# Part of VectorE's score tiles in the third bank of a score unit, and a corrected row-group duration in the planner

## The chip, the cores and the metric

The kernel runs on one core of a Trainium2 chip. Five engines work side by side: TensorE (PE for its matmuls, PEld for its weight loads), VectorE (DVE), ScalarE (ACT), GpSimd (POOL) and SyncE (SP), which issues the DMAs. Matmul results go to eight PSUM banks of 512 fp32 columns per partition. The metric is the device time of one execution in microseconds (us); lower is better.

## The reference

One pre-layernorm transformer block over 2048 tokens of width 640, in bf16: attention with 32 heads of 20 channels, then a gated GELU feed-forward (FFN) of width 1728, each with a residual.

```python
def _A_ref(x, wqkv, wo):
    qkv = (lambda x, *d: x.transpose(*d))((x @ wqkv).reshape(B, S, 3, H, Dh), 2, 0, 3, 1, 4)
    q, k, v = qkv[0], qkv[1], qkv[2]
    scores = jnp.einsum("bhqd,bhkd->bhqk", q, k) * (Dh ** -0.5)
    p = _softmax(scores, axis=-1)
    o = jnp.einsum("bhqk,bhkd->bhqd", p, v)
    return (lambda x, *d: x.transpose(*d))(o, 0, 2, 1, 3).reshape(B, S, D) @ wo
def _B_ref(x, w_gate, w_up, w_down):
    g = jnp.einsum("bsd,df->bsf", x, w_gate)
    u = jnp.einsum("bsd,df->bsf", x, w_up)
    return jnp.einsum("bsf,fd->bsd", _gelu(g) * u, w_down)
h = x + _A_ref(_layernorm(x, axis=-1), A_wqkv, A_wo)
h2 = h + _B_ref(_layernorm(h, axis=-1), B_w_gate, B_w_up, B_w_down)
```

## The kernel before

**Tiles.** The queries are cut into eight chunks (SIZES: one of 512, five of 256, two of 128 rows). Heads go in eight groups of four; the four heads of a group sit in four row groups of TensorE (32 rows each), so their score matmuls can run at the same time. A score tile is 128 keys by 512 columns of one head: one PSUM bank. A *slot* is as many head groups as fill 512 columns for a chunk (one group at 512 queries, two at 256, four at 128): 32 slots of 64 tiles, 2048 tiles in all.

**Two ways to an exponential.** Most tiles are taken in *units* that alternate between banks 0, 1, 2 and banks 3, 4 (PAT, line 829). One score operation on TensorE fills a unit's banks, and one ScalarE instruction (line 1002) takes the exponential of all of them into the probability buffers pts and pts2 (the latter a part of the buffer that the profile calls rege). The rest, D_SLOT quads of four tiles per slot, go to VectorE (d_exp, lines 880 to 908). A VectorE tile's scores are computed by a score operation of their own into a *background bank*, 7 or 5 (BG, line 1232; unit, lines 995 to 998), just behind the unit with which it is due. VectorE reads the bank (line 887), which frees it, into a quarter of a scratch tile; after four such tiles it makes four scaled copies (TERMS) that together approximate the exponential. SUMS says how many pairs of copies in a slot are added up first, so that they need one PV pass instead of two.

**PV and epilogue.** PV passes add probability times value into bank 6 (pv_op). When a slot is complete, VectorE copies bank 6 out (epilogue), and spread (lines 1021 to 1040) sends the softmax sums through four DMA hops and a reciprocal on GpSimd, multiplies on VectorE (on16, priority P_ON) and writes to the tensor attn. After the last slot of a chunk, post (line 1099) adds the output projection, the layer norm and the FFN for that chunk's rows as background work. Its accumulators use the background banks too. The FFN matmuls stand at line 674 in narrow column groups of 32 (chunks of 512 and 256 rows) and at lines 1156 and 1221 at full width (chunks of 128).

**The planner.** No order of an engine is written out by hand. Every operation is given a priority, a duration, its inputs and the banks that it takes and frees. Sched.schedule (lines 97 to 259) plays the engines forward in time and always starts the ready operation of best priority; this makes each engine's instruction order, which emit writes out with the semaphores needed. On the chip each engine follows that fixed order, whatever its real times are. What matters here: MODE_SWITCH is added on TensorE when it changes between row groups, column groups and the full array; row_start and row_end (lines 220 to 231) follow the four row groups, so that a tile for a free row group costs nearly nothing; SD_AGE (line 156) holds back a background score tile for a while so that it can join a unit; due and QK_LEAD keep background work from starting when the next unit's banks are about to come free; HOP is the time that the planner gives to one DMA hop of spread. When TensorE has nothing to do, the planner adds warm matmuls on kt_all.

Of the kernel before, what the change touches and what calls it, by code (L numbers as in the profile page):

```python
# [22 lines left out]
PE_AGE = 3.5  # L23
SD_AGE = 0.6

MODE_SWITCH = {"pe": .098, "act": 1.28}
# [20 lines left out]
class Sched:  # L49
# [47 lines left out]
    def schedule(self):  # L97
# [11 lines left out]
        mode = {e: None for e in ENGINES}  # L109
# [6 lines left out]
        t = 0.0  # L116
        recent = collections.deque()
        row_end, row_start, freed = [0.0] * 4, 0.0, [0.0] * 8
# [3 lines left out]
        scores = sum(o.eng == "pe" and o.mode == "row" for o in ops)  # L122
        while done < total:
            assert events, "no operation can start"
            t = heapq.heappop(events)
            while events and events[0] <= t + 1e-9:
                heapq.heappop(events)
            for e in ENGINES:
# [8 lines left out]
                while ready[e]:  # L137
# [10 lines left out]
                    for bk in o.acq:  # L148
# [4 lines left out]
                        else:  # L153
                            got = None
                            break
                    if got and 0 < p[0] < 1 and mode[e] != "row" and t - o.ready < SD_AGE and scores > 1:
                        skipped.append((p, i))
                        continue
# [63 lines left out]
                if o.rows:  # L222
                    if mode[e] == "row":
                        b = max([row_start + 0.01] + [freed[x.b] for x in o.acq] + [row_end[j] for j in o.rows])
                    else:
                        row_end = [0.0] * 4
                        b = t
                    row_start = b
                    for j in o.rows:
                        row_end[j] = b + 0.215  # L230
                    o.dur = max(0.012, b + 0.215 - t)
                if e == "act":
# [114 lines left out]
PR, PR2 = 12, 4  # L347
D_SLOT = (0,) + (3,) * 27 + (2,) * 2 + (1,) * 2
SUMS = (0, 1, 1, 1, 0) + (1,) * 20 + (2, 1, 0, 1, 0, 1, 0)
HOP = 2.6  # L350
D_LAT = 0.3
RECIP_MAGIC = float(0x7EF311C3)
COL = 256
VN = 6
SIX = ()
D_FIRST, D_SPAN = 0, 16
TANH_FROM = 768
# [6 lines left out]
P_KQ = 3  # L364
P_ON = 2
V_ACT = (0, 1)
# [5 lines left out]
def bass_sequential_preLN__mha_block__glu_gated_geglu__prompt_kernel(  # L372
# [12 lines left out]
    with ExitStack() as es:  # L385
# [442 lines left out]

        PAT = [((0, 1, 2), (3, 4, 5)) if c in SIX else ((0, 1, 2), (3, 4)) for c in range(len(CHUNKS))]
        d_kb, d_sums, n_sums = {}, {}, {}  # L830
# [8 lines left out]
        d_rem = {s_: [(s_,) + y + (j,) for y in ys for j in range(4)] for s_, ys in d_kb.items()}  # L839
        units, ubank, dtile, uslot = [], [], [], []  # L840
        in_slot = {}
        while rem:
            s_ = rem[0][0]
            c = slots[s_][0]
            bs = PAT[c][len(units) % 2]
            k = in_slot.setdefault(s_, [0, 0])
            nd = 4 * len(d_kb[s_])
            six = len(PAT[c][1]) == 3
            want = min(nd, (k[0] - D_FIRST) * nd // D_SPAN + 1) if k[0] >= D_FIRST and nd else 0
            xd = None  # L850
            n = len(bs)
            if k[1] < want:
                n -= six
                xd = d_rem[s_].pop(0)
                k[1] += 1
            units.append(rem[0:n])
            del rem[0:n]
            ubank.append(bs[0])
            dtile.append(xd)
            uslot.append(s_)  # L860
            k[0] += 1
# [18 lines left out]
        def d_exp(b, tile, prio):  # L880
# [7 lines left out]
                                                                 ALU.mult, ALU.max), c_dve(512), P_QK,  # L888
                            reads=[("SD", tile)], writes=[vk], rel=[b], after=aft))
            d_raw.append(tile)  # L890
# [4 lines left out]
            for i, off in enumerate(TERMS):  # L895
                a, ak = d_a[e][d_t[e] % len(d_a[e])]
                d_t[e] += 1
                d_ops.append(op("dve", I("tensor_scalar", a, v, 0.25, off, ALU.mult, ALU.add), 0.6, prio,
                                reads=[vk], writes=[ak], after=aft, lat=D_LAT))
                if i // 2 < pairs:  # L900
# [49 lines left out]
        def unit(u):  # L950
# [11 lines left out]
            xd = dtile[u]  # L962
            six = xd and len(PAT[slots[tl[0][0]][0]][1]) == 3
            al = tl + ([xd] if six else [])
# [357 lines left out]
```

## Time and profile before

| | us |
|---|---|
| median of 3 runs | 886.22 (883.67 to 892.12) |
| the profiled execution | 887.99 |
| its span, first to last instruction | 886.2 |
| TensorE's granted clock, mean | 0.998 |

The profile is of one execution. In the rows, L393 is the line of a helper that records every plain operation, so such rows are told apart by their tiles: pts<-ps and rege<-ps at 128x1024 or 128x1536 on ACT are exponentials of two or three banks, rege<-rege and qt_all<-... at 128x2048 on DVE are VectorE's scaled copies (parts of qt_all serve as scratch once their queries are used up), ps<-pts,v_all on PE is PV, on<-osb,bsum is the normalising multiply of spread. L974 is a score matmul, L887 is VectorE's read of a score bank. A timeline row merges consecutive instructions of one group: start, length to the end of the last, and in brackets how long the engine was idle before and what ended that.

### The profile page before, as it was taken

How to read it: one execution, taken by the hardware profiler on the slowest of the kernel's cores; microseconds unless marked ns; L12 is line 12 of the kernel's file. 1: busy time of each engine (PE TensorE's matmuls, PEld its weight loads, DVE VectorE, ACT ScalarE, POOL GpSimd, SP SyncE). 2: the span in 40 equal slices, each digit the busy share in tenths (PEclk: the TensorE clock that was granted, in tenths of full speed). 3: DMA queues.
4: the chain of work that ended last, by engine and by line, in shares of the span. 5: the costliest groups of instructions: out<-in, count | busy, mean ns of one | idle time of the engine just before them, and what ended most of it. 6: DMA issues, size and time to landing. Idle time of an engine off the chain costs nothing.

```text
span 886.2 us, 36314 instructions
## 1 busy us (share of the span) xinstructions
PE 839.1 (95%) x16536; PEld 416.4 (47%) x16536; DVE 746.2 (84%) x1340; ACT 838.5 (95%) x766; POOL 131.8 (15%) x431
## 2 busy tenths in 40 slices
PE   3999999999989899999999999999999999999998
PEld 1532222222234344434555555555555556666776
DVE  8838998899879988878899988899999988947753
ACT  6799999999989999999999999999999999999962
POOL 5001011110111311110031211130111211110100
PEclk9999999999999999999999999999999999999999
DMA  7211121322264510001112100201011111021000
GB/s 267 79 46 58 30 74 31 97 67 61 67 148 142 146 34 20 18 7 34 50 41 57 34 19 15 55 20 34 20 41 42 22 36 43 24 50 43 11 18 16
DMA packets 57297, 46.93 MB, mean 53 GB/s; under 512 B 25524, under 2 KB 50704, under 8 KB 57144
## 3 DMA queue, kind: packets, MB, share of 16 engines
q1 hardware_dynamic: 57144, 44.62, 19.0%
q8 instruction: 129, 2.11, 1.0%
q14 instruction: 24, 0.20, 0.1%
HBM read 30.68 MB, written 11.04 MB: 47 GB/s over the span
## 4 chain that ended last, share of the span: by engine, by line
ACT 47%; PE 41%; DVE 8%; DMA 2%; issue 1%; SPq 1%; DVEq 0%
ACT pts L393 35%; PE ps L974 13%; ACT rege L393 11%; PE ps L674 11%; PE ps L393 10%; PE ps L679 5%; PE ps L1156 1%; DVE rege L393 1%; DVE rege L887 1%; DVE stats L393 1%; PE ps L1221 1%; ACT qt_all L393 1%; DMA bsum<-rsums 1%; SPq L393 1%; DVE qt_all L393 1%
## 5 line engine op out<-in xcount | busy, mean ns | idle before, releaser
L393 ACT ACTIVATE pts<-ps 128x1024 bf16<-128x1024 f32 (+1 forms) x567 | 642.8, 1255 | 13.1 <-PE ps L974 8.1
L974 PE MATMUL ps<-qt_all,kt_all 32*128 32x256 bf16 (+2 forms) x4096 | 320.3, 273 | 15.5 <-ACT pts L393 8.8
L974 PEld LDWEIGHTS ps<-qt_all,kt_all 32*128 32x128 bf16 x4096 | 115.9, 92 | 217.1 <-ACT pts L393 110.9
L393 ACT ACTIVATE rege<-ps 128x1536 bf16<-128x1536 f32 x113 | 170.9, 1512 | 1.5 <-PE ps L974 0.9
L887 DVE TENSOR_SCALAR rege<-ps 128x512 int16<-128x512 f32 x216 | 147.4, 683 | 28.8 <-PE ps L974 27.6
L674 PE MATMUL ps<-rege,regw 128*32 128x256 bf16 (+1 forms) x3360 | 150.3, 292 | 2.0 <-DVE rege L887 0.5
L393 PE MATMUL ps<-pts,v_all 128*21 128x256 bf16 (+2 forms) x2752 | 133.7, 273 | 0.6 <-issue 0.5
L393 PE MATMUL ps<-rege,v_all 128*21 128x256 bf16 (+2 forms) x1828 | 126.2, 289 | 3.7 <-DVE rege L393 3.3
L887 DVE TENSOR_SCALAR qt_all<-ps 128x512 int16<-128x512 f32 x132 | 90.4, 685 | 23.5 <-PE ps L974 22.6
L674 PEld LDWEIGHTS ps<-rege,regw 128*32 128x32 bf16 x3360 | 79.0, 96 | 36.8 <-issue 17.6
L393 POOL TENSOR_SCALAR rn<-rc 128x16 int32<-128x16 int32 x30 | 9.3, 311 | 576.4 <-DMA rc<-sums 576.2
L393 DVE TENSOR_SCALAR rege<-rege 128x2048 int16<-128x2048 int16 x138 | 92.6, 686 | 1.5 <-PE ps L393 0.6
L679 PE MATMUL ps<-regw 128*128 128x512 bf16 (+1 forms) x360 | 87.8, 352 | 2.9 <-ACT regw L626 2.0
L393 PEld LDWEIGHTS ps<-pts,v_all 128*21 128x21 bf16 x2752 | 62.7, 92 | 32.2 <-issue 26.7
L674 PE MATMUL ps<-regw,rege 128*32 128x320 bf16 x1568 | 74.4, 301 | 1.6 <-issue 0.5
L393 DVE TENSOR_SCALAR qt_all<-qt_all 128x2048 int16<-128x2048 int16 (+3 forms) x116 | 68.2, 597 | 1.5 <-PE ps L393 0.7
L393 PEld LDWEIGHTS ps<-rege,v_all 128*21 128x21 bf16 x1828 | 48.3, 91 | 40.4 <-issue 20.3
L393 PE MATMUL ps<-qt_all,v_all 128*21 128x256 bf16 (+1 forms) x1280 | 58.0, 266 | 1.0 <-issue 0.7
L393 DVE TENSOR_SCALAR qt_all<-rege 128x2048 int16<-128x2048 int16 x80 | 54.4, 688 | 1.4 <-PE ps L393 0.7
L679 PEld LDWEIGHTS ps<-regw 128*128 128x128 bf16 x360 | 28.9, 98 | 49.9 <-issue 27.7
L674 PEld LDWEIGHTS ps<-regw,rege 128*32 128x32 bf16 x1568 | 36.1, 96 | 21.2 <-issue 10.4
L1209 DVE TENSOR_TENSOR rege<-rege,ps 128x512 bf16<-128x512 bf16 (+1 forms) x53 | 35.8, 676 | 7.6 <-PE ps L674 7.3
(115 smaller groups left out, 705.7 us busy)
## 6 DMA issues: line engine op xcount, KB each, us to landing
bsum<-rsums SPq DMA_DIRECT2D x120, 64.0 KB, 2.1
rege<-in_A_x_dram SPq DMA_DIRECT2D x5, 640.0 KB, 5.6
q_rows<-regw SPq DMA_DIRECT2D x20, 128.0 KB, 1.8
out_dram<-rege SPq DMA_DIRECT2D x16, 160.0 KB, 2.4
attn<-on SPq DMA_DIRECT2D x120, 20.0 KB
regw<-in_B_w_gate_dram SPq DMA_DIRECT2D x5, 432.0 KB, 3.4
regw<-in_B_w_up_dram SPq DMA_DIRECT2D x5, 432.0 KB, 3.2
kt_all<-k_rows SPq DMA_DIRECT2D x12, 160.0 KB
```

Of the source, the lines that this page charges most:

```text
L393: return lambda eng: getattr(eng, method)(*args, **kwargs)
L674: return [lambda eng, j=j: eng.matmul(out()[32 * j:32 * j + 32], l[:, 32 * j:32 * j + 32], r, start=start, stop=stop, tile_position=(0, 32 ...
L679: fn = col4(lambda: bank(bk, n), l, r, k == 0, k == len(steps) - 1) if col else lambda eng, l=l, r=r, k=k: eng.matmul(bank(bk, n), l, r, s ...
L887: d_ops.append(op("dve", lambda eng: eng.tensor_scalar(v[:, 512 * h:512 * h + 512], bank(b), EXP_MUL, -32000.0, ALU.mult, ALU.max), c_dve( ...
L974: return lambda eng: eng.matmul(out()[:, kk * nq:(kk + 1) * nq], kt_all[32 * j:32 * j + 32, g, kt * 128:(kt + 1) * 128], qt_all[32 * j:32 ...
L1156: lambda eng, a=a, f=f, fi=fi: eng.matmul(bank(bk)[:, fi * nq:(fi + 1) * nq], w[:, a, F0[f]:F0[f] + 128], hnT[:, a, 128 * tb:128 * tb + nq ...
L1209: hdone.append(op("dve", lambda eng, bu=bu, fv=fv, w=w: eng.tensor_tensor(fv, fv, bank(bu, w), ALU.mult), c_dve(w), p, reads=[ku] + hkeys( ...
L1221: f == NF - 1) if nq >= COL else lambda eng, f=f, o=o, hf=hf, bk=bk: eng.matmul(
```

## The change

- unit: where a VectorE tile is due in a three-bank unit, the unit may take two ScalarE tiles and have the VectorE tile in its third bank, computed in the same score operation. A list ring holds for which units this is so. D_RING gives a number per slot; out of a slot's 4 x D_SLOT tiles it spreads that many marks, and a marked tile takes the third bank if its unit has three banks; if not, it goes to a background bank as before. It replaces SIX, an empty list that would have added a sixth bank.
- d_exp: the scratch tile is tracked by quarters.
- schedule: when a score operation starts from another array mode, its rows are now counted from after the mode change and not from before it; the time of the operation itself stays the same. The rule that holds back background score tiles gets a second limit SD_ROW for when the array is in row mode.
- Constants: D_SLOT (87 to 89 quads), SUMS (28 pairs, distributed over other slots), HOP 2.6 to 3.2, P_ON 2 to 2.4, D_SPAN 16 to 18 (over how many units of a slot the VectorE tiles are spread).

Reads and writes otherwise stay as they are, but since the planner makes every order anew, all engines' orders differ from an early point on.

```diff
@@ -22,6 +22,7 @@
 QK_LEAD = .65
 PE_AGE = 3.5
 SD_AGE = 0.6
+SD_ROW = 0
 
 
 
@@ -153,7 +154,8 @@
                         else:
                             got = None
                             break
-                    if got and 0 < p[0] < 1 and mode[e] != "row" and t - o.ready < SD_AGE and scores > 1:
+                    if got and 0 < p[0] < 1 and scores > 1 and t - o.ready < (
+                            SD_AGE if mode[e] != "row" else SD_ROW if row_end[o.rows[0]] > max([row_start + 0.01] + [freed[b] for b in got]) + 0.02 else 0):
                         skipped.append((p, i))
                         continue
                     if got is None:
@@ -224,11 +226,11 @@
                         b = max([row_start + 0.01] + [freed[x.b] for x in o.acq] + [row_end[j] for j in o.rows])
                     else:
                         row_end = [0.0] * 4
-                        b = t
+                        b = t + (MODE_SWITCH[e] if mode[e] else 0.0)
                     row_start = b
                     for j in o.rows:
                         row_end[j] = b + 0.215
-                    o.dur = max(0.012, b + 0.215 - t)
+                    o.dur = max(0.012, b + 0.215 - t) - (b - t if mode[e] not in (None, "row") else 0.0)
                 if e == "act":
                     due = t + o.dur + (0.905 if o.dur > 1.2 else 1.332) - QK_LEAD if o.mode == "exp" else None
                 if o.util:
@@ -345,15 +347,15 @@
 NTERM = len(TERMS)
 PV_QUADS = 2
 PR, PR2 = 12, 4
-D_SLOT = (0,) + (3,) * 27 + (2,) * 2 + (1,) * 2
-SUMS = (0, 1, 1, 1, 0) + (1,) * 20 + (2, 1, 0, 1, 0, 1, 0)
-HOP = 2.6
+D_SLOT = (0,) + (3,) * 27 + (2, 3, 2, 1)
+SUMS = (0,) + (1,) * 6 + (0, 1, 1, 0) + (1,) * 5 + (2,) + (1,) * 10 + (0, 1, 1, 1, 0)
+HOP = 3.2
 D_LAT = 0.3
 RECIP_MAGIC = float(0x7EF311C3)
 COL = 256
 VN = 6
-SIX = ()
-D_FIRST, D_SPAN = 0, 16
+D_RING = (6,) * 26 + (4, 6, 12, 12, 0, 6)
+D_FIRST, D_SPAN = 0, 18
 TANH_FROM = 768
 GELU_A = 2.0 * 0.7978845608028654
 GELU_B = 4.0 * GELU_A * 0.044715
@@ -362,7 +364,7 @@
 P_EV = 1.8
 P_QK, P_PV, P_TAIL, P_PRO, P_EPI, P_LN, P_BG = 0, 1, 1.2, 1.5, 2, 2.5, 3
 P_KQ = 3
-P_ON = 2
+P_ON = 2.4
 V_ACT = (0, 1)
 XN_DVE = (9, 13, 15)
 V0 = 0
@@ -826,7 +828,7 @@
             tiles += [(s_, g, kb, j) for g in gs for kb in range(NT // nk) for j in range(4)]
             slot_end.append(len(tiles))
 
-        PAT = [((0, 1, 2), (3, 4, 5)) if c in SIX else ((0, 1, 2), (3, 4)) for c in range(len(CHUNKS))]
+        PAT = [((0, 1, 2), (3, 4)) for c in range(len(CHUNKS))]
         d_kb, d_sums, n_sums = {}, {}, {}
         for s_, (c, gs) in enumerate(slots):
             mine = list(dict.fromkeys(x[1:3] for x in tiles if x[0] == s_))
@@ -837,7 +839,7 @@
             n_sums[s_] = k
         rem = [x for x in tiles if x[1:3] not in d_kb[x[0]]]
         d_rem = {s_: [(s_,) + y + (j,) for y in ys for j in range(4)] for s_, ys in d_kb.items()}
-        units, ubank, dtile, uslot = [], [], [], []
+        units, ubank, dtile, uslot, ring = [], [], [], [], []
         in_slot = {}
         while rem:
             s_ = rem[0][0]
@@ -845,12 +847,12 @@
             bs = PAT[c][len(units) % 2]
             k = in_slot.setdefault(s_, [0, 0])
             nd = 4 * len(d_kb[s_])
-            six = len(PAT[c][1]) == 3
             want = min(nd, (k[0] - D_FIRST) * nd // D_SPAN + 1) if k[0] >= D_FIRST and nd else 0
             xd = None
             n = len(bs)
+            ring.append(k[1] < want and n == 3 and (k[1] + 1) * D_RING[s_] // max(nd, 1) > k[1] * D_RING[s_] // max(nd, 1))
+            n -= ring[-1]
             if k[1] < want:
-                n -= six
                 xd = d_rem[s_].pop(0)
                 k[1] += 1
             units.append(rem[0:n])
@@ -886,7 +888,7 @@
             aft = tuple(e_ops) + (tuple(last_qk[0]) if qb else ()) + (tuple(last_qk[1]) if qb > 1 else ())
             d_ops.append(op("dve", lambda eng: eng.tensor_scalar(v[:, 512 * h:512 * h + 512], bank(b), EXP_MUL, -32000.0,
                                                                  ALU.mult, ALU.max), c_dve(512), P_QK,
-                            reads=[("SD", tile)], writes=[vk], rel=[b], after=aft))
+                            reads=[("SD", tile)], writes=[vk + (h,)], rel=[b], after=aft))
             d_raw.append(tile)
             if h < 3:
                 return
@@ -896,7 +898,7 @@
                 a, ak = d_a[e][d_t[e] % len(d_a[e])]
                 d_t[e] += 1
                 d_ops.append(op("dve", I("tensor_scalar", a, v, 0.25, off, ALU.mult, ALU.add), 0.6, prio,
-                                reads=[vk], writes=[ak], after=aft, lat=D_LAT))
+                                reads=[vk + (k,) for k in range(4)], writes=[ak], after=aft, lat=D_LAT))
                 if i // 2 < pairs:
                     if i % 2 == 0:
                         m, mk = a, ak
@@ -960,7 +962,7 @@
             pb, o = (pts, p0) if p0 < PR else (pts2, p0 - PR)
             pt = pb[:, 512 * o:512 * (o + na)]
             xd = dtile[u]
-            six = xd and len(PAT[slots[tl[0][0]][0]][1]) == 3
+            six = ring[u]
             al = tl + ([xd] if six else [])
             bks = [Bank(s0 + i) for i in range(len(al))]
             fns = []
```

## The prediction

> **What bounds the kernel now.** I read the page first, then three stretches of the span, then ScalarE alone between its first and its last exponential.
>
> ```profile
> span 886.2 us, 36314 instructions
> PE 839.1 (95%) x16536; PEld 416.4 (47%) x16536; DVE 746.2 (84%) x1340; ACT 838.5 (95%) x766; POOL 131.8 (15%) x431
> ...
> ACT 47%; PE 41%; DVE 8%; DMA 2%; issue 1%; SPq 1%; DVEq 0%
> ```
>
> TensorE and ScalarE both look full, and the chain of waits runs through both. The stretches (length, then busy time of PE, PEld, DVE, ACT, POOL) part them:
>
> ```profile
> 35.70:851.00 815.30, 788.04 (x15881) 378.94 (x15881) 697.05 (x1200) 802.83 (x707) 119.66 (x399) 1.00 0.19 49
> 851.00:886.20 35.20, 30.27 (x506) 25.43 (x502) 18.75 (x44) 11.21 (x15) 0.00 (x0) 1.00 0.06 20
> ```
>
> From 35.7 to 851 ScalarE has a record open for 802.8 of 815.3 us. Behind that comes a tail of 35.2 us in which it does little and TensorE is busy for 30.3. So the time is a ScalarE stage plus a TensorE tail. ScalarE's groups in the stage (count | union of records, mean ns of one | idle before):
>
> ```profile
> L393 ACT ACTIVATE pts<-ps 128x1024 bf16<-128x1024 f32 x340 | 369.5, 1087 | 4.3 <-PE ps L393 3.3 <-PE ps L974 0.8
> L393 ACT ACTIVATE pts<-ps 128x1536 bf16<-128x1536 f32 x227 | 342.0, 1506 | 8.9 <-PE ps L974 7.3 <-PE ps L393 0.6
> L393 ACT ACTIVATE rege<-ps 128x1536 bf16<-128x1536 f32 x113 | 170.9, 1512 | 1.5 <-PE ps L974 0.9 <-PE ps L393 0.3
> L393 ACT ACTIVATE qt_all<-qt_all 128x1024 f16<-128x1024 f16 x12 | 13.3, 1111 | 1.3 <-DVE qt_all L393 1.3
> L393 ACT ACTIVATE rege<-rege 128x2048 bf16<-128x2048 bf16 x4 | 7.4, 1903 | 0.0
> L393 ACT ACT_TABLE_LOAD x4 | 5.1, 1283 | 0.1
> L393 ACT ACTIVATE qt_all<-qt_all 128x512 f16<-128x512 f16 x4 | 2.8, 703 | 0.0
> L393 ACT ACTIVATE rege<-rege 128x1536 bf16<-128x1536 bf16 x1 | 1.5, 1467 | 0.0
> L393 ACT ACTIVATE rege<-rege 128x1024 bf16<-128x1024 bf16 x1 | 1.0, 1042 | 0.0
> ```
>
> The exponentials' records add up to 882 us, more than the stage lasts: they overlap. What one costs is read from start to start in the timeline (start, length):
>
> ```profile
> 813.99 1.06 ACT L393 ACTIVATE qt_all<-qt_all 128x1024 f16<-128x1024 f16 x1 [1.27 <-DVE qt_all L393]
> 814.96 1.00 ACT L393 ACTIVATE pts<-ps 128x1024 bf16<-128x1024 f32 x1
> 815.86 1.44 ACT L393 ACTIVATE rege<-ps 128x1536 bf16<-128x1536 f32 x1
> 817.19 1.02 ACT L393 ACTIVATE pts<-ps 128x1024 bf16<-128x1024 f32 x1
> 818.10 1.07 ACT L393 ACTIVATE qt_all<-qt_all 128x1024 f16<-128x1024 f16 x1
> 819.04 3.71 ACT L393 ACTIVATE pts<-ps 128x1536 bf16<-128x1536 f32 x3
> ```
>
> Two banks cost 0.90 to 0.91 (814.96 to 815.86, 817.19 to 818.10), three banks 1.33, a tanh 0.94 us. Work in the stage: 340 x 0.905 + 340 x 1.33 + 12 x 0.94 + some 2 for the four short tanhs + 9.9 for the gelus + 5.1 for table loads = 788 us. That leaves 815.3 - 788 = 27 us of waits, and nothing that the change does to TensorE can give back more than that in the stage.
>
> **The change, part by part.** *ScalarE's load.* Going through the unit loop by hand with the new constants, the third bank is taken only where a VectorE tile is due and the unit has three banks. That is 92 of the 356 VectorE tiles, a quarter and not half. VectorE gets 8 tiles more (348 to 356), and ScalarE's exponentials become 448 of two banks, 265 of three and 1 of one, 714 instead of 680. One bank more costs 1.33 - 0.905 = 0.425, so an instruction's fixed part is 0.905 - 2 x 0.425 = 0.055 and the single-bank one costs 0.48. Sum after: 448 x 0.905 + 265 x 1.33 + 0.48 = 758.4, against 759.9 before: **-1.5 us**. The fixed part could also be read from the records: 1506 - 1087 = 419 ns a bank leaves 249 ns, and 34 more instructions would add 8.5 us instead of 1.9. I take the spacing, because 680 such records do not fit into the stage. The Trainium skill (Perfetto Trace Analysis, Optimizing Scalar/DVE Operations) speaks against this change: it asks for larger operations on a saturated engine, and puts some 51 ns of engine time on each ScalarE access to PSUM, about twice that in the profiled latency; the spacing's 55 ns agrees with it, and by the records the forecast below would be 890 instead of 883.
>
> *TensorE's load in the stage.* A score tile that finds a free row group is nearly free, one that finds none costs a pass:
>
> ```profile
> 203.74 0.39 PE L974 MATMUL ps<-qt_all,kt_all 32*128 32x512 bf16 x3
> ...
> 205.68 0.60 PE L974 MATMUL ps<-qt_all,kt_all 32*128 32x512 bf16 x4
> ...
> 799.27 0.43 PE L974 MATMUL ps<-qt_all,kt_all 32*128 32x128 bf16 x16
> ```
>
> Three tiles took 0.39, four took 0.60, and four in four groups (16 quarter-width matmuls) 0.43. In the order of the changed program, unbroken runs of four tiles fall from 159 to 90; at 0.04 to 0.21 each that saves 3 to 14 us. Twenty more runs (685 to 705) add two changes of array mode each. TensorE waits for ScalarE in the stage, so a few us either way cost nothing there; they show in how much background work is left for the tail, which is counted below from the order itself.
>
> *VectorE's load.*
>
> ```profile
> L887 DVE TENSOR_SCALAR rege<-ps 128x512 int16<-128x512 f32 x216 | 147.4, 683 | 28.8 <-PE ps L974 27.6
> L393 DVE TENSOR_SCALAR rege<-rege 128x2048 int16<-128x2048 int16 x138 | 92.6, 686 | 1.5 <-PE ps L393 0.6
> L393 DVE TENSOR_TENSOR qt_all<-qt_all 128x2048 bf16<-128x2048 bf16 x11 | 13.4, 1215 | 0.0
> ```
>
> Two quads more: 8 x 0.683 + 8 x 0.686 = 11 us on an engine with 140 us idle, hidden. Moving the summed pairs among slots leaves their number at 28. Splitting one scratch key into four changes no instruction.
>
> *The first wait.* Early in the stage ScalarE stops for a probability buffer that the first PV pass has not yet read:
>
> ```profile
> 44.13 0.61 PE L393 MATMUL ps<-pts,v_all 128*21 128x512 bf16 x8
> ...
> 44.80 3.28 ACT L393 ACTIVATE pts<-ps 128x1024 bf16<-128x1024 f32 x3 [2.98 <-PE ps L393]
> ```
>
> In the new order this PV pass stands two score units earlier, ahead of the V projections that it stood behind. Its inputs (the first eight tiles, V rows 0 and 1) are done by then: **-2.9 us**. Next in line is the score unit of that exponential, already computed.
>
> *HOP 2.6 to 3.2, P_ON 2 to 2.4.* The planner expects a transfer of the softmax sums after HOP. Where it was later, VectorE stood on the normalising multiply, with everything of its order queued behind:
>
> ```profile
> 258.60 0.69 DVE L393 TENSOR_TENSOR on<-osb,bsum 128x512 bf16<-128x512 f32 x1 [2.17 <-DMA bsum<-rsums]
> ...
> 259.95 0.61 PE L393 MATMUL ps<-rege,v_all 128*21 128x256 bf16 x8 [2.17 <-DVE rege L393]
> ...
> 261.58 1.45 ACT L393 ACTIVATE pts<-ps 128x1536 bf16<-128x1536 f32 x1 [2.58 <-PE ps L974]
> ...
> 811.60 0.69 DVE L393 TENSOR_TENSOR on<-osb,bsum 128x512 bf16<-128x512 f32 x1 [1.46 <-DMA bsum<-rsums]
> ```
>
> VectorE late, the PV pass behind it late, the next scores late: 2.58 us of ScalarE here, and 1.27 at 813.99 above. Four hops at 0.6 more are 2.4 us, over both 2.17 and 1.46: **-3.85 us**. The price is that each chunk's output projection and FFN start later, and that lands in the tail. The multiply's output transfers and the FFN's input load move behind it on SP's queue; nothing in the stage waits for them.
>
> *The tail.*
>
> ```profile
> 849.15 0.39 PE L974 MATMUL ps<-qt_all,kt_all 32*128 32x128 bf16 x8
> ...
> 854.52 3.97 PE L674 MATMUL ps<-regw,rege 128*32 128x320 bf16 x112
> ...
> 864.36 1.85 PE L1156 MATMUL ps<-rege,regw 128*128 128x128 bf16 x30 [1.20 <-DVE rege L393]
> ...
> 870.93 7.98 PE L1156 MATMUL ps<-rege,regw 128*128 128x128 bf16 x140
> ...
> 879.42 3.98 PE L1221 MATMUL ps<-regw,rege 128*128 128x320 bf16 x28 [0.52 <-DVE rege L1181]
> 883.44 0.49 DVE L1226 TENSOR_TENSOR rege<-ps,rege 128x320 bf16<-128x320 f32 x1 [1.34 <-PE ps L1221]
> ```
>
> Behind the last score pass (849.15) TensorE works almost without a break to 883.4. In the new order it has more to do there: 224 instead of 124 narrow down-projection matmuls and 140 gate/up matmuls of 256 columns instead of none. 112 of the former took 3.97 less the 0.2 by which a record outlasts its stream, 0.134 for a group of four, so 25 groups are 3.35; at 256 columns a group takes 4/5 of that, and 35 of them are 3.75. Together +7.1. They fill the waits of this tail (1.20 and 0.52, and about 0.4 that the list does not single out): **+5.0 us**.
>
> *What no row shows:* the third bank of such a unit is now handed back by VectorE. From the end of a score pass it has about two exponentials, 2 x 0.905 = 1.81 us; the longest operation it can be caught in is 1.22 and its own read 0.68, 1.90 in all, and the score pass still has half a us in hand after that. So it costs nothing while VectorE keeps to the plan; the other end is five stalls of the size seen at 261.58, 13 us. Below nothing the end is the 27 - 6.8 = 20 us of waits left, if freed background banks removed them all. I take 0, by the arithmetic.
>
> The planner's corrected row-group duration moves only the order, which is counted above. SD_ROW is 0, and no waiting time is below 0, so the new clause of the age rule never holds.
>
> **Sum:** -1.5 - 2.9 - 3.85 + 5.0 = -3.3 us. The profiled execution took 887.99, its span and 1.8 us around it, which is 1.8 above the median of the three runs, 886.22. Taken off the median: **883 us**.
>
> **Rivals.** *Slower: the handed-back bank.* VectorE runs at 85%, in a fixed order; where it is behind, the three-bank score pass waits, and PV and FFN queued behind it on TensorE wait too, the path of 258.60 to 261.58. The bound is passed at 12 us over the forecast: 0.13 us on each of 92 units, or five such stalls. At 0.2 each it gives 901. Against it: before, VectorE stood idle 28.8 us in front of 216 of its reads, waiting for scores. Chance 0.19.
>
> *Faster: the small waits go.* If the 264 tiles left in two background banks, instead of 348, and 69 fewer four-tile passes halve the 20 us of scattered waits, 873. For it: in each of those waits a score pass came late. Against it: ScalarE's recorded idle time in its main groups is only 14.7 us, most of it already spent above. Chance 0.24.
>
> *The repairs do not hold, the tail stays:* hops longer than 3.2, or another wait in place of the first. Then -1.5 + 5.0 and part of the rest: 886 to 890. Chance 0.15.
>
> **How the numbers follow.** The forecast has 0.42. About 1% is what a measurement of this kernel can tell from no change (its runs reach from 883.67 to 892.12): below 877.4 is faster, above 895.1 slower. Forecast and third rival lie within: 0.57; faster 0.24, slower 0.19. The range 873 to 897 reaches to the second rival and a little into the first; its own range for the likeliest case is 878 to 889.
>
> **What would show it.** 714 exponentials with starts 0.905 and 1.33 apart; no wait near 3 us at 42 to 45; no multiply waiting over 1 us for its sums; the last exponential near 843, with about 40 us behind it. ScalarE waits behind VectorE's reads, or a stage still of 815 us, would make it wrong.

## The result, and the profile after

| | before | changed |
|---|---|---|
| median of 20 runs each, one chip | 887.17 (883.67 to 894.76) | 885.08 (882.42 to 888.09) |
| ratio, with its 95% interval | | 0.9965 [0.9948, 0.9982] |
| the profiled execution / its span | 887.99 / 886.2 | 884.74 / 883.0 |

The ratio is worth 3.1 us (1.6 to 4.6); the medians differ by 2.1. The prediction's sum was 3.3.

Part of this goes with TensorE's granted clock. In the profiled execution of the kernel before, TensorE ran at half clock from 259.6 to 263.1 us. It had stood idle for 2.17 us until 259.95, and the half clock covers most of the stall up to 261.58 that the prediction put down to the softmax sums alone. This is its row of that window (the third number from the end is the granted clock):

```profile
259.60:263.10 3.50, 3.15 (x48) 1.28 (x48) 1.59 (x3) 1.45 (x1) 0.00 (x0) 0.51 0.53 164
```

The changed kernel's trace has no such stretch before the end, and 18 of its 20 runs have a mean clock of 1.000 (median 885.1 us). The clocks of the 20 runs of the kernel before are not on record, save the profiled one's (0.998). Of its 57 runs beside the experiments 17 have 1.000, with medians of 886.2, 886.1 and 885.5 us in the three groups, and at 0.998 these are 1.3 to 2.1 us higher. So at the same clock some 0.4 to 1.1 us of the gain are left. Whether the changed order is what keeps the clock up is open: kernels 2 and 12 below, close relatives of it, have no run at 1.000, and kernel 1, on the chip of kernel 2, has all of its twelve there.

The page of the changed kernel (busy time and share of each engine, then the chain of waits):

```profile
span 883.0 us, 36651 instructions
...
PE 830.0 (94%) x16658; PEld 405.4 (46%) x16658; DVE 753.4 (85%) x1356; ACT 832.0 (94%) x798; POOL 134.2 (15%) x431
...
ACT 56%; PE 28%; DVE 12%; POOL 1%; issue 1%; DMA 1%
```

TensorE's busy time is 9 us less than before, ScalarE's 6.5 less, and the chain runs over ScalarE for 56% instead of 47%. The stretches of the changed kernel, cut at its last exponential (length, then PE, PEld, DVE, ACT, POOL):

```profile
35.70:842.00 806.30, 771.72 (x15818) 361.86 (x15820) 701.20 (x1211) 798.76 (x740) 122.05 (x399) 1.00 0.19 49
842.00:883.00 41.00, 37.53 (x704) 31.51 (x695) 22.83 (x52) 8.61 (x14) 0.00 (x0) 1.00 0.05 18
```

ScalarE's groups of exponentials in the changed kernel (count | union of records, mean ns | idle before):

```profile
L395 ACT ACTIVATE pts<-ps 128x1024 bf16<-128x1024 f32 x406 | 426.6, 1119 | 2.6 <-PE ps L976 1.4 <-PE ps L395 1.0
L395 ACT ACTIVATE pts<-ps 128x1536 bf16<-128x1536 f32 x178 | 273.1, 1535 | 5.5 <-PE ps L976 4.8 <-PE ps L395 0.6
L395 ACT ACTIVATE rege<-ps 128x1536 bf16<-128x1536 f32 x87 | 133.7, 1537 | 1.6 <-PE ps L395 1.5
...
L395 ACT ACTIVATE rege<-ps 128x1024 bf16<-128x1024 f32 x42 | 44.9, 1120 | 0.0
...
L395 ACT ACTIVATE pts<-ps 128x512 bf16<-128x512 f32 x1 | 0.7, 668 | 0.0
```

That is 448 of two banks, 265 of three, 1 of one, as counted. ScalarE's timeline at the three places that the prediction named (start, length):

```profile
37.02 4.63 ACT L395 ACTIVATE pts<-ps 128x1536 bf16<-128x1536 f32 x4 [3.58 <-PE ps L976]
...
42.84 3.33 ACT L395 ACTIVATE pts<-ps 128x1024 bf16<-128x1024 f32 x3
46.46 2.37 ACT L395 ACTIVATE pts<-ps 128x1536 bf16<-128x1536 f32 x2 [0.29 <-PE ps L395]
...
256.51 1.67 ACT L395 ACTIVATE rege<-ps 128x1536 bf16<-128x1536 f32 x1
257.84 5.35 ACT L395 ACTIVATE pts<-ps 128x1024 bf16<-128x1024 f32 x5
262.91 1.63 ACT L395 ACTIVATE rege<-ps 128x1536 bf16<-128x1536 f32 x1
...
841.39 0.67 ACT L395 ACTIVATE pts<-ps 128x512 bf16<-128x512 f32 x1
842.07 1.28 ACT L395 ACT_TABLE_LOAD   x1
```

The wait of 2.98 us at 44.80 is gone (the 0.29 at 46.46 stands before a later instruction, where the kernel before waited 0.24), the 2.58 at 261.58 is gone, and the last exponential, of a single bank at 0.48 us, counts until 841.9 (850.9 before). VectorE's wait for the softmax sums in the changed kernel, by the list of waits (total us, times, longest):

```profile
DVE on L395 <- DMA bsum<-rsums: 0.6, 2, 0.4
```

Before, this line read 4.0 us in 3 waits. Behind the last exponential, TensorE's long groups and the last instruction of the changed kernel:

```profile
842.45 2.95 PE L676 MATMUL ps<-rege,regw 128*32 128x256 bf16 x88
...
849.86 6.84 PE L676 MATMUL ps<-regw,rege 128*32 128x320 bf16 x196
...
861.15 6.96 PE L1158 MATMUL ps<-rege,regw 128*128 128x128 bf16 x119
...
876.18 3.98 PE L1223 MATMUL ps<-regw,rege 128*128 128x320 bf16 x28 [0.52 <-DVE rege L1183]
...
880.19 0.49 DVE L1228 TENSOR_TENSOR rege<-ps,rege 128x320 bf16<-128x320 f32 x1 [1.34 <-PE ps L1223]
```

So the 3.2 us between the two spans come together thus. The stage runs from the first exponential's start to the last one's start plus its spacing. It shrank from 815.1 to 804.9. By the spacings its work is 786.5 instead of 788.0, so its waits fell from 27.1 to 18.4. The tail grew from 35.4 to 41.1, and the stage began 1.3 later (37.02 against 35.72). -10.2 + 5.7 + 1.3 = -3.2.

### The profile page after: what moved, and what is told of

Read it like the earlier page. It is cut to its first block, busy times and chain, and to the rows that moved or that the text cites. A ratio compares the mean times of both kernels' runs of the same rounds, so it can differ in the third digit from the quotient of the medians.

```text
span 883.0 us, 36651 instructions
## 1 busy us (share of the span) xinstructions
PE 830.0 (94%) x16658; PEld 405.4 (46%) x16658; DVE 753.4 (85%) x1356; ACT 832.0 (94%) x798; POOL 134.2 (15%) x431
## 4 chain that ended last, share of the span: by engine, by line
ACT 56%; PE 28%; DVE 12%; POOL 1%; issue 1%; DMA 1%
ACT pts L395 44%; ACT rege L395 12%; PE ps L676 9%; PE ps L976 7%; PE ps L395 5%; PE ps L681 4%; DVE qt_all L395 3%; DVE rege L889 2%; PE ps L1158 2%; DVE rege L395 2%; DVE qt_all L889 1%; DVE stats L395 1%; PE ps L1223 1%; DMA rege<-xn_t 1%; ACT qt_all L395 1%
## 5 line engine op out<-in xcount | busy, mean ns | idle before, releaser
L976 PE MATMUL ps<-qt_all,kt_all 32*128 32x256 bf16 (+2 forms) x4096 | 301.2, 272 | 24.3 <-ACT pts L395 17.5
L976 PEld LDWEIGHTS ps<-qt_all,kt_all 32*128 32x128 bf16 x4096 | 101.8, 92 | 227.1 <-ACT pts L395 150.5
L395 ACT ACTIVATE rege<-ps 128x1536 bf16<-128x1536 f32 (+1 forms) x129 | 178.6, 1401 | 1.7 <-PE ps L395 1.5
L676 PE MATMUL ps<-rege,regw 128*32 128x256 bf16 (+1 forms) x3360 | 152.4, 292 | 5.7 <-ACT rege L395 1.8
L395 PE MATMUL ps<-rege,v_all 128*21 128x256 bf16 (+2 forms) x1877 | 130.1, 287 | 2.3 <-issue 1.5
L681 PE MATMUL ps<-regw 128*128 128x512 bf16 (+1 forms) x360 | 90.2, 356 | 2.5 <-ACT regw L628 2.0
L395 PEld LDWEIGHTS ps<-pts,v_all 128*21 128x21 bf16 x2711 | 62.4, 91 | 30.1 <-issue 23.3
L395 DVE TENSOR_SCALAR qt_all<-qt_all 128x2048 int16<-128x2048 int16 (+2 forms) x118 | 68.8, 594 | 0.6
L395 PEld LDWEIGHTS ps<-rege,v_all 128*21 128x21 bf16 x1877 | 50.1, 91 | 36.4 <-issue 20.9
L395 DVE TENSOR_SCALAR qt_all<-rege 128x2048 int16<-128x2048 int16 x83 | 56.2, 689 | 1.6 <-PE ps L395 1.0
```

Source lines behind the costliest of these rows:

```text
L395: return lambda eng: getattr(eng, method)(*args, **kwargs)
L676: return [lambda eng, j=j: eng.matmul(out()[32 * j:32 * j + 32], l[:, 32 * j:32 * j + 32], r, start=start, stop=stop, tile_position=(0, 32 ...
L681: fn = col4(lambda: bank(bk, n), l, r, k == 0, k == len(steps) - 1) if col else lambda eng, l=l, r=r, k=k: eng.matmul(bank(bk, n), l, r, s ...
L976: return lambda eng: eng.matmul(out()[:, kk * nq:(kk + 1) * nq], kt_all[32 * j:32 * j + 32, g, kt * 128:(kt + 1) * 128], qt_all[32 * j:32 ...
```

## The experiments

Twelve kernels ran, in groups that each shared their own runs of the kernel before; so the ratios are to be compared, not the medians. "On PV" is the part of the stage's waits in which a probability buffer was not free yet, by the list of waits; the last three columns are one profiled execution each, worked out as above.

| kernel | median us | ratio to before | waits in the stage | on PV | tail |
|---|---|---|---|---|---|
| before | | 1 | 27.1 | 4.2 | 35.4 |
| changed | 885.08 | 0.9965 [0.9948, 0.9982] | 18.4 | 3.1 | 41.1 |
| 1 changed, without the correction | 890.55 | 1.0022 [1.0001, 1.0043] | 23.6 | 5.0 | 42.0 |
| 2 changed, old HOP and P_ON | 889.04 | 1.0014 [0.9989, 1.0039] | 23.3 | 2.1 | 39.6 |
| 3 changed, exponentials split | 899.96 | 1.0108 [1.0063, 1.0153] | 19.8 | 1.8 | 40.9 |
| 4 changed, no third bank | 902.99 | 1.0175 [1.0143, 1.0207] | 40.7 | 15.8 | 39.7 |
| 5 changed, third bank wherever it can be | 895.44 | 1.0081 [1.0053, 1.0109] | 30.2 | 6.5 | 39.3 |
| 6 before, quarter keys | 892.43 | 1.0043 [1.0020, 1.0067] | 23.9 | 5.6 | 41.2 |
| 7 before, quarter keys, third bank | 898.46 | 1.0103 [1.0064, 1.0143] | 30.0 | 11.9 | 38.1 |
| 8 before, new HOP and P_ON | 897.83 | 1.0106 [1.0065, 1.0146] | 29.2 | 3.2 | 41.7 |
| 9 changed, no third bank, D_SPAN 16 | 900.13 | 1.0112 [1.0074, 1.0150] | 27.3 | 2.1 | 54.1 |
| 10 changed, D_SPAN 16 | 898.41 | 1.0092 [1.0055, 1.0128] | 32.2 | 13.3 | 40.2 |
| 11 before, quarter keys, correction | 897.71 | 1.0093 [1.0057, 1.0129] | 31.5 | 3.0 | 41.7 |
| 12 changed, HOP 3.1 | 885.94 | 0.9945 [0.9918, 0.9972] | 21.2 | 2.0 | 40.3 |

**1. Without the planner's correction.**

```diff
-                        b = t + (MODE_SWITCH[e] if mode[e] else 0.0)
+                        b = t
...
-                    o.dur = max(0.012, b + 0.215 - t) - (b - t if mode[e] not in (None, "row") else 0.0)
+                    o.dur = max(0.012, b + 0.215 - t)
```

> The changed kernel with the planner's row-group duration as before the change. My theory (the correction is what moved the first PV pass ahead, and nothing else of size): in the order the first PV pass stands behind 18 score tiles again instead of 13, so ScalarE waits some 3 us for a probability buffer at 42 to 45 us, and 1.6 us more background streaming lies behind the last score pass (37.3); time 888 to 890. Rival (the correction only reshuffles): 885, no wait over 1 us at that place.

ScalarE's timeline of this kernel:

```profile
40.79 1.45 ACT L395 ACTIVATE rege<-ps 128x1536 bf16<-128x1536 f32 x1
45.23 1.02 ACT L395 ACTIVATE pts<-ps 128x1024 bf16<-128x1024 f32 x1 [2.99 <-PE ps L395]
```

The first wait is back at its old length, and it is 3 of the 5.2 us by which the stage's waits grew. That the correction moved the first PV pass is shown; kernel 11 has the correction as well, and its longest wait on PV is 1.0 us.

**2. The old HOP and P_ON.**

```diff
-HOP = 3.2
+HOP = 2.6
...
-P_ON = 2.4
+P_ON = 2
```

> The changed kernel with HOP back at 2.6 and P_ON back at 2. My theory (the larger HOP bought the waits of VectorE on the softmax sums and paid for them in the tail): waits of the normalising multiply on its sums come back, 2 to 5 us in all with one over 1 us and a wait of ScalarE behind it; the tail behind the last exponential is 3 to 4 us shorter, because 4.3 us less background streaming stands behind the last score pass in the order (31.4 instead of 35.7); time 884 to 886, the same within 0.2% as the changed kernel's 885.1. Rival (in the new order nothing waits on the sums any more, HOP only delayed the background work): no such wait, tail 4 us shorter, time 881.

VectorE's wait for the sums in this kernel:

```profile
DVE on L395 <- DMA bsum<-rsums: 1.7, 2, 1.0
```

Up from 0.6 us, and the stage waits 4.9 us longer, but not for the sums. VectorE waits for them 0.65 us at 277.4 and 1.05 at 532.9, and ScalarE's timeline has no wait behind either. 4.8 us of its waits stand together at another place, where TensorE waited for the normalised rows of an FFN (the transfer rege<-xn_t) and then ran at half clock (the window's row comes first):

```profile
311.60:318.40 6.80, 5.81 (x74) 2.14 (x78) 2.91 (x6) 3.08 (x3) 2.79 (x10) 0.50 0.41 113
...
312.59 0.62 PE L676 MATMUL ps<-rege,regw 128*32 128x512 bf16 x4 [2.58 <-DMA rege<-xn_t]
...
313.79 2.36 ACT L395 ACTIVATE pts<-ps 128x1536 bf16<-128x1536 f32 x2 [2.81 <-PE ps L976]
...
317.68 1.02 ACT L395 ACTIVATE pts<-ps 128x1024 bf16<-128x1024 f32 x1 [1.52 <-PE ps L976]
```

In the changed kernel the same load costs ScalarE 1.0 us (at 313.63), without half clock. So the two constants keep VectorE from waiting on the sums, but that this is worth the forecast 3.85 us is not shown. All 12 runs here have a mean clock below 1.000; against runs of the kernel before at the same clock this kernel is 1.0 to 1.8 us faster (889.0 to 890.1 at 0.996, 886.5 to 888.3 at 0.998). The tail got only 1.5 us shorter, where some 4 us less work was left for it.

**3. Each three-bank exponential as two instructions**, of two banks and of one: the same elements, 265 instructions more.

```diff
-            exp_ops.append(op("act", I("activation", pt, PS[:, 512 * s0:512 * s0 + n], ACT.Exp, scale=SCALE),
+            cut = 1024 if na == 3 else n
+            exp_ops.append(op("act", [I("activation", pt[:, a:b], PS[:, 512 * s0 + a:512 * s0 + b], ACT.Exp, scale=SCALE)
+                                      for a, b in ((0, cut), (cut, n)) if b > a],
```

> The changed kernel with each three-bank exponential written as two instructions, two banks and one, in the same place of the same order: 266 single-bank instructions more, nothing else changed, same result. By the spacing (0.055 us fixed part each) ScalarE's work grows by 265 x 0.055 = 14.6 us, and the time with it by 10 to 16 us, to 895 to 901, less only what falls into its 18 us of waits; the two parts start 0.905 and 0.48 apart. By the records (249 ns fixed part each) it would grow by 66 us, to 950.

By the ratios it is 12.7 us slower than the changed kernel ((1.0108 - 0.9965) x 887), its stage 15.9 longer (820.8 against 804.9): 0.048 to 0.060 us for each instruction. The starts of the parts lie 0.90 and 0.48 apart. The spacing's 0.055 holds; the records' 0.249 would have been 66 us. The Trainium skill (Perfetto Trace Analysis, Optimizing Scalar/DVE Operations) names some 51 ns for ScalarE's access to PSUM; this run agrees.

**4. No third bank.** All of VectorE's tiles go through the background banks again.

```diff
-D_RING = (6,) * 26 + (4, 6, 12, 12, 0, 6)
+D_RING = (0,) * 32
```

> The changed kernel with D_RING all 0: every VectorE tile goes to a background bank as before, all else as changed (677 exponentials instead of 714). My theory (the third bank itself is worth nothing; the gain is the two repaired waits): ScalarE's work 756.0 instead of 758.4, background streaming behind the last score pass 34.0 instead of 35.7, so 882 to 885, not slower than the changed kernel; the first wait stays away. Rival (relief of the background banks is the gain): 888 or more, with scattered waits of ScalarE in the stage back from some 18 to 25 us or more.

My theory, that the third bank was worth nothing, fell: this is the slowest of all, with 22 us more waits in the stage than the changed kernel. Two places carry them. Its list of waits on PV:

```profile
ACT pts L395 <- PE ps L395: 10.9, 11, 2.0
...
ACT rege L395 <- PE ps L395: 4.9, 3, 2.3
```

And one stall by itself, in the timeline of SP's queue, TensorE and ScalarE:

```profile
137.48 0.32 SPq L395 DMA_DIRECT2D bounds<-regw  x1
...
141.80 0.59 SPq L395 DMA_DIRECT2D qt_all<-bounds  x1
...
144.29 0.60 PE L976 MATMUL ps<-qt_all,kt_all 32*128 32x512 bf16 x6
...
144.73 1.45 ACT L395 ACTIVATE rege<-ps 128x1536 bf16<-128x1536 f32 x1 [8.05 <-PE ps L976]
```

The queries of the later head groups are prepared as background work: projected (line 681), their bounds computed (line 777) and sent through DRAM into qt_all. The scores of the next head group need them; here ScalarE got these scores 8 us late. TensorE was not idle meanwhile: it worked through PV passes, warm matmuls and, from 140.98 to 144.3, projections that stand ahead of these scores in its order. So it is the order that has the scores late, and that it does so for this transfer is read from the program, not shown by a wait.

**5. The third bank wherever a due tile finds a three-bank unit** (196 exponentials of three banks are left).

```diff
-D_RING = (6,) * 26 + (4, 6, 12, 12, 0, 6)
+D_RING = (12,) * 32
```

> The changed kernel with D_RING all 12: every VectorE tile that is due in a three-bank unit takes the third bank; 748 exponentials, 552 of two banks and 196 of three, 759.7 us of ScalarE work by the spacings instead of 758.4. My theory (VectorE hands the bank back in time, the third bank costs only the fixed part of more exponentials): no wait of a score pass on VectorE's read of more than 0.5 us in a way that recurs, the stage 1 to 2 us longer, the tail 5 us shorter because 29.5 instead of 35.7 us of background streaming stands behind the last score pass: 880 to 883. Rival (the handed-back bank stalls the score passes): twice as many such units, twice the stalls; at 0.1 to 0.2 us on each of 100 more units 890 or more.

Missed by over 12 us: the stage waits 11.8 us longer than in the changed kernel, in many pieces of 0.2 to 0.9 us, and the tail got 1.8 shorter instead of 5. The slower time is the rival's, but not by its path: by the list of waits the score passes waited 1.8 us for VectorE's reads of scores, against 4.5 in the changed kernel. What makes the pieces was not separated.

**6. The kernel before with the scratch tile tracked by quarters**, alone.

```diff
-                            reads=[("SD", tile)], writes=[vk], rel=[b], after=aft))
+                            reads=[("SD", tile)], writes=[vk + (h,)], rel=[b], after=aft))
...
-                                reads=[vk], writes=[ak], after=aft, lat=D_LAT))
+                                reads=[vk + (k,) for k in range(4)], writes=[ak], after=aft, lat=D_LAT))
```

> The kernel before with one edit alone: VectorE's scratch tile tracked by quarters. It is the pair to the next run, which adds the third bank to it. On the chip VectorE's four reads of a quad stand in one order either way, so only the planner's order differs. Both theories: no repair of the first wait (the first PV pass stands behind 18 score tiles as before), the multiply can wait on its sums again, background streaming behind the last score pass 34.3 us (before: 28.2), so 888 to 893.

As expected. No instruction is added, the orders are made anew, and the tail grows by 5.8 us while the stage loses 3.2 of waits: a tail as long as the changed kernel's comes with this edit alone.

**7. The same, with the third bank**, all other constants as before (D_SPAN 16).

```diff
-D_RING = (0,) * 32
+D_RING = (6,) * 26 + (4, 6, 12, 12, 0, 6)
```

> The run before plus the third bank with D_RING as in the change; constants, planner duration and slots as in the kernel before. Theory A (relief: without the third bank a VectorE tile waits for one of two shared background banks, its quad ends late, the slot's last PV pass comes late, and ScalarE waits for probability buffers): at least 5 us faster than the run with the keys alone, 880 to 886, ScalarE's waits on PV other than the first one under 2 us. Theory B (what cost 18 us when the third bank was taken out of the changed kernel was an accident of that order, an 8 us wait for late queries above all): within 3 us of the run with the keys alone once the shorter tail (27.3 us of background streaming instead of 34.3) is taken off.

Slower again than kernel 6, by 0.6%, where the theory of freed background banks asked for faster. The waits on PV are 11.9 us, 3.0 of them the old first wait; the others recur about every 50 us, such as the one in its timeline of ScalarE and VectorE:

```profile
393.34 3.28 ACT L395 ACTIVATE pts<-ps 128x1536 bf16<-128x1536 f32 x3 [1.54 <-PE ps L395]
393.56 0.69 DVE L395 COPY osb<-ps 128x512 f32<-128x512 f32 x1 [0.82 <-PE ps L395]
```

The copy of bank 6, which ends a slot, waits beside it: the slot's last PV passes are late.

**8. The kernel before with the new HOP and P_ON**, alone.

```diff
-HOP = 2.6
+HOP = 3.2
...
-P_ON = 2
+P_ON = 2.4
```

> The kernel before with HOP 3.2 and P_ON 2.4 alone. My theory: no wait of the multiply on its sums over 1 us (before: 2.2 and 1.5), so ScalarE's waits of 2.58 and 1.27 go, and 35.8 instead of 28.2 us of background streaming lies behind the last score pass: -3.9 + 5 to 7, 888 to 891, not faster than before. Rival (it is worth its 4 us by itself): 883 to 885.

VectorE's wait for the sums is gone from the list altogether, and still the kernel is 1% slower than before: other stalls came, one of 2.71 us at 142, and a tail of 41.7. The repair does what it is for, and by itself it does not pay.

**9. and 10. The third bank against D_SPAN**, over how many units of a slot VectorE's tiles are spread. Kernel 9:

```diff
-D_RING = (6,) * 26 + (4, 6, 12, 12, 0, 6)
-D_FIRST, D_SPAN = 0, 18
+D_RING = (0,) * 32
+D_FIRST, D_SPAN = 0, 16
```

> The changed kernel with D_RING all zero and D_SPAN back at 16. Theory A (without the third bank, VectorE's tiles spread over 18 units come too late for the end of the slot): ScalarE's row of waits on PV falls from the 15.8 us of the run with D_RING zero alone to under 5; the order leaves 9.8 us more background work behind the last score pass, so 890 to 898. Theory B (the 18 us of that run were an accident of one plan, D_SPAN has no part): PV waits stay above 10 us, and with the longer tail 905 to 912.

Kernel 10 keeps the third bank:

```diff
-D_FIRST, D_SPAN = 0, 18
+D_FIRST, D_SPAN = 0, 16
```

> The changed kernel with D_SPAN 16 instead of 18, the third bank kept. Theory A (a wider spread only delays the end of a slot): waits on PV stay at the 2 us of the changed kernel or fall, and the order leaves 5.8 us less behind the last score pass: 879 to 884. Theory B (the constants hold each other: third bank with 16 crowds VectorE, as in the run of the third bank with the old constants): PV waits near 12 us, 890 to 897.

The waits on PV in the list of kernel 9:

```profile
ACT pts L395 <- PE ps L395: 1.6, 2, 1.3
...
ACT rege L395 <- PE ps L395: 0.5, 1, 0.5
```

and of kernel 10:

```profile
ACT pts L395 <- PE ps L395: 13.3, 19, 1.6
```

For PV, theory A held in kernel 9 and theory B in kernel 10. The two constants go together: 18 without the third bank costs 15.8 us (kernel 4), 16 with it 13.3 (and 8.9 beyond the first wait in kernel 7), and the matched pairs, the changed kernel and kernel 9, 2 to 3. A slot has some 21.2 units without the third bank (677 exponentials in 32 slots) and 22.3 with it (714). So 18 of 21.2 probably brings VectorE's last quads late, with the slot's last PV pass and the copy of bank 6 behind them. Why 16 of 22 is bad as well stays open. Kernel 9 is slower than forecast (890 to 898), by its tail of 54 us and by the stall of kernel 4, again:

```profile
140.97 0.32 SPq L395 DMA_DIRECT2D bounds<-regw  x1
...
144.24 0.59 SPq L395 DMA_DIRECT2D qt_all<-bounds  x1
...
147.91 1.45 ACT L395 ACTIVATE rege<-ps 128x1536 bf16<-128x1536 f32 x1 [10.93 <-PE ps L976]
```

**11. The kernel before with quarter keys and the correction.** The edit is the first one, the other way round, on kernel 6.

> The kernel before with the quarter keys and the corrected row-group duration alone. If the parts add up: the first wait of 3 us is gone, the tail's background work is 1.5 us longer than with the quarter keys alone, multiply waits stay near 4 us: 889 to 892. If what a new plan does by chance outweighs the parts: outside of 887 to 894, with waits at places that the kernel before does not have.

The first wait is gone, and the stall is there a third time:

```profile
141.28 0.32 SPq L395 DMA_DIRECT2D bounds<-regw  x1
142.84 0.58 SPq L395 DMA_DIRECT2D qt_all<-bounds  x1
...
147.92 1.45 ACT L395 ACTIVATE rege<-ps 128x1536 bf16<-128x1536 f32 x1 [9.79 <-PE ps L976]
```

The time fell outside of what adding the parts gives, by a stall that recurs. In the changed kernel the same transfers read:

```profile
127.47 0.32 SPq L395 DMA_DIRECT2D bounds<-regw  x1
129.08 0.59 SPq L395 DMA_DIRECT2D qt_all<-bounds  x1
```

and in the kernel before:

```profile
119.95 0.32 SPq L393 DMA_DIRECT2D bounds<-regw  x1
```

All fourteen traces sort by it. With the correction and the third bank this transfer starts at 122.5 to 129.1 (six kernels, no stall). With the correction and without the third bank it starts at 137.5 to 141.3 (4, 9, 11; stalls of 8 to 11 us). Without the correction it starts at 120 to 122, save for kernel 8, the new HOP without the third bank: 134.6, with its stall of 2.71 us. Start less stall gives an estimate of the time by which it has to go: 129 to 132 in these four. So two of the edits delay this preparation, and the third bank keeps it in time. That it does so by leaving the background banks to it (264 of VectorE's tiles in them instead of 356) is the likely reason; it was not tried by itself.

**12. HOP 3.1 instead of 3.2**, a control: nothing but a new order.

```diff
-HOP = 3.2
+HOP = 3.1
```

> The changed kernel with HOP 3.1 instead of 3.2, a step with no reason of its own to cost or gain in the stage; only the order is made anew. If times follow from the mechanisms: multiply waits near 1 us, first wait absent, 4.6 us less background work behind the last score pass, 880 to 885. If a new plan of itself moves the time by several us: above 888 or below 878, with ScalarE's waits in the stage 5 us or more away from the 18 of the changed kernel.

Its interval overlaps the changed kernel's. The waits in the stage are 2.8 us more, about as much as ScalarE waits in and beside a stretch of half clock from 307.5 to 314.3 us; the tail is 0.8 us less where the count of the order promised 4.6. A new order of itself is worth a few us here and not the 11 to 19, by the ratios, of kernels 4 and 7 to 11. Neither this kernel nor any other is shown to beat the changed one.

## Why the prediction was right

The forecast gain of 3.3 us met a measured 3.1, but partly by luck: the waits were read from an execution with a stretch of half clock, which the prediction did not look at, and at the same clock some 0.4 to 1.1 us of the gain are left. The 883 itself lies 2 us under the measured 885.1; it was taken off 886.22, the median of three runs, and twenty gave 887.17.

- **ScalarE's load, -1.5.** The counts came out as worked out by hand, and kernel 3 shows that the price of an instruction is the spacing's.
- **The first wait, -2.9.** Gone, and kernel 1 brings it back. The gain is shown to be the correction's, which the prediction had filed under the order alone.
- **HOP and P_ON, -3.85.** The waits for the sums went from 4.0 to 0.6 us, and no wait stands at either place named; the longest multiply wait is 0.4 us. The path is the one forecast, the size is not shown: kernel 2 brings back 1.1 us of these waits with none of ScalarE behind them, and the larger part of the term, the 2.58 us at 261.58, lay for the most part in a stretch of half clock.
- **The tail, +5.0.** It grew by 5.7, and the stage ended at 841.9 where "near 843" was forecast. The size holds, the rule behind it does not carry far: in kernels 2, 5, 10 and 12 the orders leave 4.3 to 6.2 us less behind the last score pass, and the tails are 0.8 to 1.8 shorter. The amount of background work is not all that sets it.
- **The handed-back bank, 0.** Against the kernel before, the sum closes without it: the waits fell by 8.7 us where first wait and HOP together promise 6.75, so it costs nothing that shows and may have given 2; no run separates that from the HOP term. The slower rival found no place: by the lists of waits, the score passes waited less for VectorE's reads into rege, first before, then after (total us, times, longest); for those into qt_all it was 3.1 and 2.0 us:

```profile
PEld ps L974 <- DVE rege L887: 7.1, 26, 0.5
```

```profile
PEld ps L976 <- DVE rege L889: 2.5, 7, 0.5
```

But 0 is not what the third bank is worth. Among the new constants, leaving it out costs 2.1% (kernel 4 against the changed one); among the old ones, putting it in costs 0.6% (7 against 6). The prediction took the parts one by one against the kernel before and added them. Here that gave nearly the measured total, and it did read the tail from the complete order of the changed program; no part that was tried alone behaved so. Every one that ran alone (6, 8), or beside the quarter keys only (7, 11), is slower than before.
- **The faster rival** (small waits halve) did not come: beside the two repairs, the waits went from about 20 us to 18.4.
- **Not foreseen:** the stage began 1.3 us later. Among the kernels the first exponential starts anywhere from 35.7 to 37.0; what decides it was not looked for.

## What to carry to other kernels

Where a planner makes one fixed order, the edits of a change are not terms that add: judge each in the company it ships with, and read the sum from the complete new order. A constant that spreads work over units has to move when the number of units does (D_SPAN with the third bank: 2 to 3 us of waits against 13 to 16). And a resource that shows in no wait of the engine that bounds, as the background banks before, can still be what keeps another edit affordable: follow the deadlines of the background work (here one transfer that, by the estimate above, must start by about 130) before giving it the value nothing. Last, look at the granted clock of every run before a difference of 0.3% is explained: here the larger part of the difference goes with it.

## What the runs showed of the hardware

ScalarE's records and its real cost part ways more than expected: the records of two- and three-bank exponentials suggest 0.249 us for an instruction by itself, and 265 more of them cost 0.048 to 0.060 each. The same small transfer is not equally fast each time: this row of the changed kernel sums up its seven transfers into the tensor bounds.

```profile
DMA to landing us min/median/max: 1.4/1.5/3.5
```

TensorE's clock was not the same in every run. A mean of 0.998 is one stretch of 3.5 us at half clock in this span of 886 us, and in the kernel before one such step went with 1.3 to 2.1 us. In the traces of the kernel before and of kernel 2 the stretch begins while TensorE stands idle for 2.17 and 2.58 us; in the changed kernel's stage its longest idle time was 1.29 us, and there was no half clock. In kernel 12 the stretch begins 0.7 us after an idle time of 1.28 us, so the length of one idle time does not decide it. What does was not tried.
